# Attention weights of two batches transposed by TensorE in float32, those of two by DMA in float16, and all four worked off two heads at a time

## The chip, the cores and the metric

The kernel runs on one core of one Trainium2 chip. The metric is device time in microseconds (us), from the start of the program to its end. The kernel before took 1043.95 us, the median of three runs (1043.25 to 1050.18). The engines are named as in the profile: PE is TensorE, DVE is VectorE, ACT is ScalarE, POOL is GpSimd, SP is SyncE, which issues the DMAs.

## The reference

Three parts follow one another. The first is attention for B = 4 batches, H = 8 heads, S = 576 tokens and D = 64, with a memory term:

```python
scores = q @ k.T / sqrt(D)                    # causal: keys after the query get -1e9
a = exp(scores - scores.max(-1)); a /= a.sum(-1) + 1e-9
local = a @ v
q_p = where(q > 0, q, exp(q) - 1) + 1
mem_out = (q_p @ M_prev) / (q_p @ z_prev + 1e-6)
g = 1 / (1 + exp(-beta))                      # one number for each head
attn = g * mem_out + (1 - g) * local
```

Its output, 2304 tokens of 512 numbers, goes through two feed-forward layers with 512 inputs and 2048 hidden units: `(s * relu(x @ w_in)**2 + b) @ w_out`, and `(max(h, 0) + alpha * min(h, 0)) @ w_out` with `h = x @ w_in`. All inputs and the output are float32.

## The kernel before

**Order.** The program is not written in the order in which it runs. Each piece of work is handed to a planner (`Plan`, lines 68 to 254) by `op`, with an engine, a guessed duration, the keys it reads and writes, and a priority. `Plan.order` then lays out one fixed order for every engine's queue: whenever an engine is free it takes the ready piece of the highest priority. Attention comes ahead of feed-forward work (`ATT`, `MOE`, line 284), and the conversion of the first layer's weights ranks with batch 2 (`WP`, line 868). Some pieces may go to ACT or DVE (`either`, line 406), whichever is free first. The SBUF buffers are slots of 640 float32 columns, given out while the order is made: 15 for all (`NSLOT`, line 39), and 12 more in the room of the last four weight tiles, which batch 0 and the first weights use (`early`).

**Attention, batches 0 and 1** (`EXACT`, line 44; `pair`, line 628). Two heads lie one above the other in the 128 partitions, 64 rows each. The queries are cut into five chunks (`PAIRED`, line 33) in two sets, (0, 1) and (2, 3, 4) (`PSETS`). For each chunk PE makes the float32 scores of both heads (lines 680 and 692), DVE adds the mask and finds the largest (line 666), ACT takes the exponentials and their sums (line 658). Then the weights are scaled and split into a high float16 part on ACT (line 730) and what is left, the low part, on DVE (line 734). SP transposes both by a DMA (line 750), five of them for each pair of heads. PE multiplies them with the values, split in the same way (high by high, high by low, low by high, lines 761 to 765), into the lower and upper column half of a PSUM bank for the two heads, on top of the memory term (`remembered`, line 617, a float32 matmul against the identity). One copy brings the set out (lines 774 to 778).

**Attention, batches 2 and 3** (`head`, line 795). One head at a time, with keys and queries loaded twice, one copy above the other. Both are split into two float32r parts (lines 804 to 809), so that the 128 rows hold high and low keys and two matmuls make the scores (lines 813 and 814). Weights are again split into two float16 parts (lines 577 to 583), transposed by DMA (line 590) and multiplied (line 606). The memory term is written first (`recall`, line 780), and the local part is added onto it in two DVE instructions for each set (line 835).

For every pair of heads `values` (line 419) loads the values, sums their absolute values on ACT (line 435), spreads the sum by a small matmul (line 437) and makes the two float16 parts with that scale (lines 447 and 450). `features` (line 455) makes `q_p` and the memory term (lines 479 to 490).

**Feed-forward.** Layer 1 runs in seven blocks of tokens (512, 320, 320, then four of 288), layer 2 in five (four of 512, one of 256). Each block has 16 steps of 128 hidden units. A step has 12 matmuls into the hidden units (lines 945 to 947) and 12 into the output (lines 979 to 981), in two float32r parts with three products each. A block of layer 1 starts when the attention output of its tokens is stored (line 858) and loaded again (line 1035), and split (lines 1045 and 1047). The weights are loaded by step and converted by four DVE and one ACT instruction for each half (lines 889 to 905). PSUM has eight banks: four for the output sums, one for hidden units, two for scores and one for attention output (lines 339 to 343); in batch 0 the scores use six and the output two (line 393).

```python
ring = {"S": ["S0", "S1"], "O": ["O"]}[kind] + (spare[kind] if b == 0 else [])
```

Of the kernel before, what the change touches and what calls it, by code (L numbers as in the profile page):

```python
# [26 lines left out]
CHUNKS = [(0, 64), (64, 128), (192, 128), (320, 128), (448, 128)]  # L27
SETS = [(0, 1, 2), (3, 4)]

GROUPS = [[(0,), (1, 2)], [(3,), (4,)]]  # L30


PAIRED = [(128, 256), (128, 384), (128, 128), (128, 512), (64, 576)]
AT = [0, 128, 256, 384, 512]
PSETS = [(0, 1), (2, 3, 4)]
NC = len(CHUNKS)
NKB = 5
GW = 640
NSLOT = 15

XS = 7
RES = dict(t=0, fq=7, fe=1, fa=0, k=7, q=0, v=7, vf=6, p=1, w=2, xt=2, st=6, st2=4, wb=3, x=0)
W1GATE = 1
EXACT = (0, 1)
YS = 4
XF = 4
KG = 2
# [5 lines left out]
FLEX = 'x'  # L53
WP = 2.0
LIFT = 2.0 ** 14
# [4 lines left out]
class Slot:  # L60


    def __init__(self, reserve, early=False, size=1, above=0):
        self.reserve, self.early, self.size, self.above = reserve, early, size, above
        self.place, self.left, self.end = None, 0, 0.0


class Plan:
# [49 lines left out]
    def order(self):  # L118
# [12 lines left out]
        places = range(self.nslots + self.nextra)  # L131
# [19 lines left out]
        def spot(t, s):  # L151

            if s.early:
                for x in reversed(places[self.nslots + s.above:]):
                    if is_free(x, t) and (s.size == 1 or (x - self.nslots) % 3 < 2 and is_free(x + 1, t)):
                        return x
# [5 lines left out]
            return min(base, key=lambda x: place_free[x], default=None)  # L162

        gone = set()
        while len(out) < n:
# [21 lines left out]
            while avail[e]:  # L187
# [4 lines left out]
                new = [s for s in o[6] if s.place is None]  # L192
                if all(spot(t, s) is not None for s in new) and all(x in closed or not taken[x] and place_free[x] <= t for x in o[8]):
                    pick = c[1]
                    break
                closing.update(x for x in o[8] if x < self.nslots)
# [14 lines left out]
            closed.update(claim)  # L211
            for s in slots:
                if s.place is None:
                    s.place = spot(t, s)
                    for x in range(s.place, s.place + s.size):
                        taken[x] = True
# [13 lines left out]
            if nbytes:  # L230
                dma_free = max(dma_free + (110.0 if dur < 500 else 30.0), t + min(dur, 625.0) + 650.0) + nbytes / (360.0 if dur < 500 else 290.0)
                done[i] = dma_free + 900.0
# [35 lines left out]

def t_dve(n, rate=1.04, extra=0.0):
    return 69 + n * rate + extra  # L270
# [6 lines left out]
def build(tc, kd, kp, qd, vd, qp, mzd, beta8, sb2, win1, wout1, win2, wout2, alpha, outT):  # L277
# [8 lines left out]
    with tc.tile_pool(name="sb", bufs=1) as sb, tc.tile_pool(  # L286
# [30 lines left out]
        qh = sb.tile([128, S], F32R, name="qh")  # L317
        ql = sb.tile([128, S], F32R, name="ql")
        ks = sb.tile([128, S], F32R, name="ks")
        vsc = sb.tile([128, 2, 6], F32, name="vsc")  # L320
        allone = sb.tile([128, 128], F32, name="allone")
        mz = sb.tile([128, NP, MZ], F32, name="mz")
# [3 lines left out]
        mx = sb.tile([128, 2, NC + 1], F32, name="mx")  # L326
        sm = sb.tile([128, 2, NC + 1], F32, name="sm")
        mxp = sb.tile([128, 2, 10], F32, name="mxp")
        smp = sb.tile([128, 2, 10], F32, name="smp")
        nrm = sb.tile([128, 6], F32, name="nrm")  # L330
        wsc = sb.tile([128, H + 9 * NP], F32, name="wsc")
        bgc = sb.tile([128, H], F32, name="bgc")
        bsc = sb.tile([128, H + 9 * NP], F32, name="bsc")
# [23 lines left out]
        op("SP", 475, lambda: nc.sync.dma_start(out=bsc, in_=beta8), w=["bsc"], bytes_=512 * (H + 9 * NP), prio=-6)  # L357
# [12 lines left out]
        op("POOL", 300, lambda: nc.gpsimd.memset(sm, 1.0), w=[("sm", j, g) for j in range(2) for g in range(2)])  # L370

        op("POOL", 100, lambda: nc.gpsimd.memset(one, 1.0), w=["one"])

        def consts():

            A.activation(out=wsc, in_=bsc, func=AF.Exp)
            A.activation(out=bgc, in_=bsc[:, 0:H], func=AF.Exp, scale=-1.0)

        def consts2():
            V.tensor_scalar(out=wsc, in0=wsc, scalar1=1.0, scalar2=1.0 / LIFT, op0=ALU.add, op1=ALU.mult)  # L380
# [10 lines left out]
        cnt = {"ch": 0, "S": 0, "O": 0}  # L391

        spare = {"S": [("Y", d) for d in range(YS)], "O": ["H"]}

        def next_bank(b, kind):
            ring = {"S": ["S0", "S1"], "O": ["O"]}[kind] + (spare[kind] if b == 0 else [])
            cnt[kind] += 1
            return ring[cnt[kind] % len(ring)]


# [17 lines left out]

        def values(b, p):
# [3 lines left out]
            sv, sf = Slot(RES["v"], early), Slot(RES["vf"], early)  # L423
            tot, un, sc, gg = vsc[:, j, 0:1], vsc[:, j, 1:2], vsc[:, j, 2:3], vsc[:, j, 4:6]
            bk = next_bank(b, "S")
# [7 lines left out]
            op("SP", 475, lambda: nc.sync.dma_start(out=at(sv, n), in_=vd[b, p]),  # L433
               r=gate(b * H + 2 * p, KV, KV0), prio=-7 if b + p == 0 else None, w=[sv], bytes_=512 * n)
            op("ACT", t_act(n, 93, 180), lambda: A.activation(out=at(sf, n), in_=at(sv, n), func=AF.Abs, accum_out=tot),
               r=[sv], w=[sf, ("tot", j)])
            op("PE", 100, lambda: T.matmul(bank_of[bk][:, 0:1], allone, tot, start=True, stop=True),
# [3 lines left out]
                out=un, in0=bank_of[bk][:, 0:1], scalar1=2.0 ** -100, scalar2=LIFT ** -2, op0=ALU.max, op1=ALU.mult),  # L441
# [4 lines left out]
                out=gg, in0=bgc[:, 2 * p:2 * p + 2], scalar1=un, scalar2=None, op0=ALU.mult), r=[("un", j), "bgc"], w=[("gg", j)])  # L446
# [713 lines left out]
```

## Time and profile before

| | |
|---|---|
| median of three runs | 1043.95 us (1043.25 to 1050.18) |
| profiled execution | 1047.11 us, span 1045.2 us |
| PE busy | 998.5 us (96%) |
| DVE busy | 672.1 us (64%) |
| ACT busy | 498.7 us (48%) |
| POOL busy | 19.2 us (2%) |
| moved by DMA | 109.45 MB, 105 GB/s in the mean |

The span runs from the first instruction to the last. A busy share is an average over the whole span; the stages differ, so the rows below also cut it into stretches. Records of matmuls that follow one another overlap, since the next one starts while the last drains; a distance between two starts is what a matmul costs in a row of them. A float32 matmul shows as two records.

### The profile page before, as it was taken

What the parts mean: (1) busy time and instruction counts of PE and PEld (TensorE: products, weight loads), DVE (VectorE), ACT (ScalarE), POOL (GpSimd) and SP (SyncE); (2) the same over time, 40 slices, a digit from 0 to 9 for tenths busy, and PEclk for the clock granted to TensorE, in tenths of its full rate; (3) what the DMA queues carried; (4) which work ended last, traced back from release to release, by engine and by line L of the source; (5) the groups of instructions that cost most, each with busy time, mean ns of one, the idle gap of its engine ahead of it and who ended that gap; (6) DMA issues with size and microseconds to landing.
All of it is one profiled execution on the core that took longest, in us unless ns stands there. A gap on an engine that the chain in (4) does not pass through costs nothing.

```text
span 1045.2 us, 17420 instructions
## 1 busy us (share of the span) xinstructions
PE 998.5 (96%) x6544; PEld 866.4 (83%) x6544; DVE 672.1 (64%) x1607; ACT 498.7 (48%) x1198; POOL 19.2 (2%) x102
## 2 busy tenths in 40 slices
PE   6767999999999999999999999999999999999998
PEld 4544777768999999999999999888888888888898
DVE  6898998668678768667744367888434534433344
ACT  7774677568767777776644554222211211211111
POOL 1000000000000000000000000000000000000000
PEclk9865999998999999999999999999999999999999
DMA  5998856475456456455341134332200200100010
GB/s 166 202 222 261 243 134 196 112 187 128 116 126 134 117 131 155 91 133 128 74 169 41 64 121 164 101 122 90 81 1 1 71 1 1 40 1 1 1 41 21
DMA packets 150500, 109.45 MB, mean 105 GB/s; under 512 B 118160, under 2 KB 125328, under 8 KB 150416
## 3 DMA queue, kind: packets, MB, share of 16 engines
q1 hardware_dynamic: 150416, 108.34, 38.7%
q8 instruction: 51, 0.84, 0.3%
q14 instruction: 33, 0.27, 0.1%
HBM read 65.85 MB, written 14.16 MB: 77 GB/s over the span
## 4 chain that ended last, share of the span: by engine, by line
PE 79%; DVE 5%; DMA 5%; ACT 2%; issue 1%; SPq 1%; ACTq 0%; DVEq 0%
PE yb L979 12%; PE yb L980 12%; PE yb L981 12%; PE hb L945 7%; PE hb L946 7%; PE hb L947 7%; PE sp L945 3%; PE sp L947 3%; PE sp L946 3%; PE ob L606 2%; PE ob L945 2%; PE ob L947 2%; PE ob L946 2%; DMA pool<-pool 1%; PE sp L813 1%
## 5 line engine op out<-in xcount | busy, mean ns | idle before, releaser
L979 PE MATMUL yb<-gr,wt 128*128 128x288 f32 (+4 forms) x608 | 204.8, 337 | 0.2 <-ACT pool L1004 0.2
L980 PE MATMUL yb<-gr,wt 128*128 128x288 f32 (+4 forms) x608 | 200.3, 330 | 0.0
L981 PE MATMUL yb<-gr,wt 128*128 128x288 f32 (+4 forms) x608 | 200.1, 329 | 0.0
L945 PE MATMUL hb<-xr,wt 128*128 128x288 f32 (+3 forms) x528 | 176.6, 334 | 0.7 <-ACT gt L959 0.5
L946 PE MATMUL hb<-xr,wt 128*128 128x288 f32 (+3 forms) x528 | 171.1, 324 | 0.0
L947 PE MATMUL hb<-xr,wt 128*128 128x288 f32 (+3 forms) x528 | 170.9, 324 | 0.0
L967 ACT CAST gr<-gt 128x288 fp32r<-128x288 f32 (+3 forms) x152 | 75.1, 494 | 141.0 <-DVE gt L965 134.2
L968 DVE TENSOR_TENSOR gr<-gt,gr 128x288 fp32r<-128x288 f32 (+3 forms) x152 | 81.2, 534 | 76.3 <-ACT gr L967 75.2
L979 PEld LDWEIGHTS yb<-gr,wt 128*128 128x128 f32 x608 | 114.6, 189 | 12.0 <-issue 3.3
L981 PEld LDWEIGHTS yb<-gr,wt 128*128 128x128 f32 x608 | 114.6, 188 | 8.5
L980 PEld LDWEIGHTS yb<-gr,wt 128*128 128x128 f32 x608 | 114.7, 189 | 7.8
L945 PEld LDWEIGHTS hb<-xr,wt 128*128 128x128 f32 x528 | 100.2, 190 | 12.1 <-issue 5.3
L947 PEld LDWEIGHTS hb<-xr,wt 128*128 128x128 f32 x528 | 100.1, 190 | 5.8
L946 PEld LDWEIGHTS hb<-xr,wt 128*128 128x128 f32 x528 | 100.4, 190 | 5.0
L959 ACT ACTIVATE gt<-hb 128x288 f32<-128x288 f32 (+2 forms) x112 | 49.7, 444 | 98.2 <-PE hb L947 95.4
L967 ACT CAST qh<-mz 128x512 fp32r<-128x512 f32 (+1 forms) x40 | 23.1, 578 | 143.7 <-DVE mz L965 143.6
L981 PE MATMUL yb<-ql,wt 128*128 128x512 f32 (+1 forms) x160 | 59.6, 372 | 0.0
L945 PE MATMUL sp<-xr,wt 128*128 128x512 f32 (+1 forms) x160 | 59.4, 371 | 0.0
L947 PE MATMUL sp<-xr,wt 128*128 128x512 f32 (+1 forms) x160 | 59.4, 371 | 0.0
L946 PE MATMUL sp<-xr,wt 128*128 128x512 f32 (+1 forms) x160 | 59.4, 371 | 0.0
L980 PE MATMUL yb<-qh,wt 128*128 128x512 f32 (+1 forms) x160 | 59.2, 370 | 0.0
L979 PE MATMUL yb<-qh,wt 128*128 128x512 f32 (+1 forms) x160 | 59.1, 369 | 0.1
(306 smaller groups left out, 1823.4 us busy)
## 6 DMA issues: line engine op xcount, KB each, us to landing
pool<-win SPq DMA_DIRECT2D x19, 512.0 KB, 4.4
pool<-wout SPq DMA_DIRECT2D x15, 512.0 KB, 3.7
room<-wout SPq DMA_DIRECT2D x14, 512.0 KB, 4.7
room<-win SPq DMA_DIRECT2D x11, 512.0 KB, 4.1
pool<-y SPq DMA_DIRECT2D x18, 256.0 KB, 3.6
out_t<-pool SPq DMA_DIRECT2D x16, 256.0 KB, 2.0
pool<-qd SPq DMA_DIRECT2D x12, 288.0 KB, 3.2
pool<-kd SPq DMA_DIRECT2D x10, 288.0 KB, 3.4
```

The lines of the kernel that those rows point to most:

```text
L606: T.matmul(obk[:, q0 - o0:q0 - o0 + nq], W[:, kb, pw], P[:, x, 0:nq], start=(first and kb == x == 0), stop=False, skip_group_check=True)
L813: T.matmul(sp, qh[:, q0:q0 + 128], ks[:, k0:k0 + kn], start=True, stop=False)
L945: T.matmul(H_, W_h, X_h, start=(d == 0), stop=False)
L946: T.matmul(H_, W_h, X_l, start=False, stop=False)
L947: T.matmul(H_, W_l, X_h, start=False, stop=(d == KD - 1))
L959: op("ACT", t_act(n, 50), lambda: A.activation(out=t_, in_=H_, func=AF.Relu), r=[hk, "gr"], w=[tk], prio=-1)
L967: op("ACT", t_act(n), lambda: A.copy(out=G_h, in_=t_), r=[tk], w=[("gh", gj)], prio=-1)
L968: op("DVE", t_dve(n), lambda: V.tensor_tensor(out=G_l, in0=t_, in1=G_h.bitcast(F32), op=ALU.subtract), r=[tk, ("gh", gj)], w=[("gl", gj)], ...
L979: T.matmul(Y, W_h, G_h, start=(f == 0), stop=False)
L980: T.matmul(Y, W_l, G_h, start=False, stop=False)
L981: T.matmul(Y, W_h, G_l, start=False, stop=(f == KF - 1))
```

## The change

- `WHOLE = (0, 1)`: in batches 0 and 1 the weights stay float32. They are scaled in place (ACT or DVE), transposed by PE in blocks of 128 columns into a PSUM bank, up to four blocks at a time, and copied back (ACT or DVE) over the place they came from. The products are float32 against the values as loaded. The split of the values, their sum and the scale fall away there.
- Batches 2 and 3 are worked off by `pair` too, two heads at a time, with two float16 parts, DMA transposes and three products, as batches 0 and 1 were before. `scores`, `turn`, `products`, `remembered`, `recall` and `head` are gone, and so are the doubled keys and queries.
- The memory term is brought in by matmuls with `is_transpose`, in the same instruction group as all products of a set.
- PSUM banks are no longer dealt round: the planner gives them out like slots (`Bank`), all eight in batch 0 and three later. A piece of PE work also takes the slot that its exponentials will fill (`room_for`).
- `NSLOT` is 17 instead of 15; the reserves, guessed durations and DMA rates of the planner change; layer 2's first weight load, and no longer its first token load, claims the slots that layer 2's split tokens take over.

```diff
-EXACT = (0, 1)
+WHOLE = (0, 1)
+class Bank(Slot):
+    def __init__(self, banks):
+        super().__init__(0)
+        self.banks = banks
+        def bank_for(b):
+            return Bank(range(8) if b == 0 else range(3))
+        def bank_at(bk):
+            return banks[bk.place - NSLOT - 3 * XF]
...
+            if b in WHOLE:
+                return sv                    # values: no sum, no parts
...
+        def turn_whole(b, g, j, cs, ch0, sp, sw, weights_of):
...
+                    either("x", t_act(nk, 93, 93), lambda p_c=p_c, sc=sc, nk=nk: A.activation(
+                        out=p_c(0, nk), in_=p_c(0, nk), func=AF.Copy, scale=sc),
+                        t_dve(nk, 0.52, 60), lambda p_c=p_c, sc=sc, nk=nk: V.tensor_scalar(
+                        out=p_c(0, nk), in0=p_c(0, nk), scalar1=sc, scalar2=None, op0=ALU.mult), r=[("sm", j, g, col)], w=wk)
...
+                    for k0 in range(0, nkb, 3 if nkb == 5 else 4):
+                        n = min(3 if nkb == 5 else 4, nkb - k0)
+                        bk = bank_for(b)
+                        def mm(p_c=p_c, k0=k0, n=n, bk=bk):
+                            for i in range(n):
+                                T.transpose(bank_at(bk)[:, 128 * i:128 * i + 128], p_c(128 * (k0 + i), 128), ident)
...
+                        either("x", t_act(128 * n, 50), lambda p_t=p_t, k0=k0, n=n, bk=bk: A.copy(
+                            out=p_t(k0, n), in_=bank_at(bk)[:, 0:128 * n]),
+                            t_dve(128 * n), lambda p_t=p_t, k0=k0, n=n, bk=bk: V.tensor_copy(
+                            out=p_t(k0, n), in_=bank_at(bk)[:, 0:128 * n]), r=[bk], w=[(s, c, k0, "t")])
...
+                turned = (turn_whole if b in WHOLE else turn_parts)(b, g, j, cs, ch0, sp, sw, weights_of)
+                ok = bank_for(b)
+                def mm(cs=cs, turned=turned, o0=o0, ok=ok):
+                    obk = bank_at(ok)
+                    for c in cs:
+                        nq = CHUNKS[c][0]
+                        r = 128 - nq
+                        T.matmul(obk[:, AT[c] - o0:AT[c] - o0 + nq], at(sa, 2 * D * NC)[r:, 2 * D * c:2 * D * c + 2 * D],
+                                 ident[r:, r:], is_transpose=True, start=(c == cs[0]), stop=False, skip_group_check=True)
...
+                        for kb in range(nkb):
+                            for w, k in ((0, kb),) if b in WHOLE else ((0, kb), (1, kb), (0, nkb + kb)):
                                 for odd in (1, 0):
+                                    _, p_t, y = turned[odd, c]
+                                    T.matmul(obk[D * odd:D * odd + D, AT[c] - o0:AT[c] - o0 + nq], W[:, kb, odd, w],
+                                             p_t(k)[:, y:y + nq], start=False, stop=False, skip_group_check=True)
...
-                if b in EXACT:
-                    pair(b, p, sp_, sa, sf, xt)
-                else:
-                    recall(b, p, sa, xt)
-                    head(b, 2 * p, sf, xt)
-                    head(b, 2 * p + 1, sf, xt)
+                pair(b, p, sp_, sa, sv, xt)
```

`turn_parts` holds the splitting and the DMA transposes that `pair` had before (lines 712 to 752).

## Rows read from the trace of the kernel before

**Rows 1.** The page, part 1: busy us (share of the span) and instructions of each engine.
```profile
PE 998.5 (96%) x6544; PEld 866.4 (83%) x6544; DVE 672.1 (64%) x1607; ACT 498.7 (48%) x1198; POOL 19.2 (2%) x102
```

**Rows 2.** Stretches: length, then each engine's busy us (instructions), PE clock, DMA share, GB/s.
```profile
0.00:67.20 67.20, 48.37 (x454) 32.78 (x455) 54.51 (x189) 53.32 (x145) 3.09 (x17) 0.90 0.80 194
67.20:95.50 28.30, 16.25 (x122) 11.35 (x121) 24.53 (x66) 15.70 (x37) 0.20 (x1) 0.51 0.95 253
...
105.10:226.00 120.90, 118.22 (x781) 87.35 (x781) 100.95 (x252) 83.09 (x186) 0.61 (x3) 1.00 0.61 166
226.00:245.10 19.10, 14.51 (x115) 11.38 (x115) 12.54 (x38) 12.41 (x33) 0.84 (x5) 0.82 0.67 202
...
545.00:1045.20 500.20, 496.20 (x2628) 428.54 (x2628) 258.73 (x426) 120.10 (x235) 0.00 (x0) 1.00 0.15 51
```

**Rows 3.** Timeline, end of batch 0: start us, us, engine, line, operation [idle before].
```profile
67.06 0.20 ACT L658 ACTIVATION_READ_ACCUMULATOR room<-yb,mxp 128x1 f32 x1
...
73.21 0.81 DVE L734 SCALAR_TENSOR_TENSOR room<-room,smp,room 128x576 f16<-128x576 f32 x1
...
72.00 5.59 SPq L750 DMA_TRANSPOSE room<-room  x3
...
83.89 0.33 SPq L858 DMA_DIRECT2D x<-room  x1
...
87.37 0.42 SPq L1035 DMA_DIRECT2D poolx<-x  x1
...
95.54 0.79 PE L945 MATMUL hb<-xr,wt 128*128 128x512 f32 x1
```

**Rows 4.** Stretch 0 to 67.2 us, instructions of line 734 alone (busy on DVE).
```profile
0.00:67.20 67.20, 16.13 (x31) 0.90 0.80 194
```

**Rows 5.** The same stretch, instructions of line 730 alone (busy on ACT).
```profile
0.00:67.20 67.20, 15.47 (x31) 0.90 0.80 194
```

**Rows 6.** Single lines: engine, operation xcount: ns min/median/max, first and last start, shapes.
```profile
L450 DVE SCALAR_TENSOR_TENSOR poolx<-poolx,vsc x4: 855/866/881, 59.9 to 487.6; 128x640 f16<-128x640 f32 x4
L447 ACT ACTIVATE poolx<-poolx,vsc x4: 828/829/832, 53.1 to 484.7; 128x640 f16<-128x640 f32 x4
L435 ACT ACTIVATE poolx<-poolx x4: 727/732/732, 35.0 to 460.0; 128x640 f32<-128x640 f32 x4
L891 DVE TENSOR_SCALAR pool<-pool x31: 416/421/428, 49.9 to 725.2; 128x512 int32<-128x512 int32 x31
L1013 DVE COPY pool<-yb x10: 424/690/692, 732.7 to 1041.7; 128x512 f32<-128x512 f32 x8, 128x256 f32<-128x256 f32 x2
```

**Rows 7.** Timeline of PE, batch 1: bundles of attention matmuls at full clock.
```profile
206.59 0.49 PE L680 MATMUL sp<-pool,poolx 64*128 64x128 f32 x4
...
210.64 1.13 PE L680 MATMUL sp<-pool,poolx 64*128 64x512 f32 x4
...
215.82 0.88 PE L617 MATMUL ob<-ident,pool 128*128 128x128 f32 x6 [0.18 <-ACT poolx L774]
216.63 0.70 PE L692 MATMUL sp<-pool,poolx 64*64 64x288 f32 x4
...
227.65 1.03 PE L764 MATMUL ob<-poolx,pool 128*64 128x128 f16 x30 [1.21 <-DMA poolx<-pool]
...
229.07 0.66 PE L764 MATMUL ob<-pool 128*64 128x64 f16 x30 [0.39 <-DMA pool<-poolx]
```

**Rows 8.** Timeline of PE, batch 2: scores and products of one head between feed-forward matmuls.
```profile
290.27 0.38 PE L813 MATMUL sp<-ks,qh 128*128 128x288 f32 x1
290.49 0.30 PE L814 MATMUL sp<-ks,ql 128*128 128x288 f32 x1
290.62 0.31 PE L945 MATMUL hb<-xr,wt 128*128 128x320 f32 x1
...
291.32 0.73 PE L606 MATMUL ob<-poolx,pool 128*128 128x128 f16 x10
291.86 0.40 PE L945 MATMUL hb<-xr,wt 128*128 128x320 f32 x1
```

More of the change, by code (lines that the diff above doesn't have):

```diff
@@ L130, in order @@
         done = [0.0] * n
-        places = range(self.nslots + self.nextra)
+        places = range(self.nslots + self.nextra + 8)
         place_free = [0.0 for _ in places]
@@ L162, in spot, with take @@
             return min(base, key=lambda x: place_free[x], default=None)
+        def take(t, new):
+            for k, s in enumerate(new):
+                s.place = spot(t, s)
+                if s.place is None:
+                    for u in new[:k]:
+                        for x in range(u.place, u.place + u.size):
+                            taken[x] = False
+                        u.place = None
+                    return False
+                for x in range(s.place, s.place + s.size):
+                    taken[x] = True
+            return True
         gone = set()
@@ L191, in order @@
                 o = self.ops[c[1]]
[L192 to L196, printed above, removed]
+                if all(x in closed or not taken[x] and place_free[x] <= t for x in o[8]):
+                    closed.update(o[8])
+                    if take(t, [s for s in o[6] if s.place is None]):
+                        pick = c[1]
+                        break
+                else:
+                    closing.update(x for x in o[8] if x < self.nslots)
                 skipped.append(c)
@@ L210, in order @@
             eng, dur, fn, deps, prio, nbytes, slots, late, claim = self.ops[i]
[L211 to L216, printed above, removed]
             if e == "PE":
@@ L389, in build @@
            r=["ident"], w=["ident"])
[L391 to L398, printed above, removed]
+        cnt = {"ch": 0}
+        banks = [sbank[0], sbank[1], obank, hbank] + ybank
+        def bank_for(b):
+            return Bank(range(8) if b == 0 else range(3))
+        def bank_at(bk):
+            return banks[bk.place - NSLOT - 3 * XF]
         def gate(hg, ahead, ahead0):
@@ L593, in products @@
-        def products(g, part, parts, turned, sf, obk, ok, first=False):
-            pw, c = part
-            q0, nq, nk, pk, p_c, ch = parts[part]
-            tk, p_t = turned[part]
-            nkb = c + 1
-            o0 = CHUNKS[SETS[g][0]][0]
-            def mm():
-                P = p_t()
-                W = at(sf, 2 * NKB * 2 * D, FP16).rearrange("p (n h e) -> p n h e", h=2, e=2 * D)
-                for kb in range(nkb):
-                    for x in (kb, nkb + kb):
-                        T.matmul(obk[:, q0 - o0:q0 - o0 + nq], W[:, kb, pw], P[:, x, 0:nq],
-                                 start=(first and kb == x == 0), stop=False, skip_group_check=True)
-            op("PE", 2 * nkb * t_b(nq), mm, r=[tk, sf], w=[ok], prio=ATT + ch * 10 + 1)
@@ L677, in pair @@
+                    room_for = [(weights_of(c, odd)[0], c, "s") for odd in range(2)]
                     if c < NC - 1:
@@ L846, in attention @@
                 plan.lean = VLEAN
-                sf = values(b, p)
+                sv = values(b, p)
                 plan.lean = FLEAN
```

453 lines of the change are left out of this document (166 added, 287 removed).

## Prediction

> **What bounds the kernel now.** I read the whole span first, then the stretches, then the few rows at the joints between them. Over the span PE is busy 96% of the time [rows 1]. That is an average over stages with different limits, so the stretches decide [rows 2]. From 545 us to the end PE is busy 496 of 500 us at full clock, on feed-forward matmuls alone. From 105 to 226 us, where the first feed-forward block shares PE with batch 1, it is busy 118 of 121 us. Behind 105 us, then, the time is PE work, and a microsecond of PE work taken out or put in there is a microsecond of the kernel. Two places are different. Up to 67 us DVE (54.5 of 67.2 us) and ACT (53.3) set the pace while PE has room. And between 226 and 245 us PE is idle 4.6 us and runs at a mean clock of 0.82.
>
> The joint at the start is in [rows 3]. The last exponentials of batch 0 end at 67.3 us; its last low weight part is made on DVE at 73.2 to 74.0; SP issues three transposes in 72.0 to 77.6; the last store of batch 0 is issued at 83.9, the load of the same rows at 87.4, and the first feed-forward matmul starts at 95.5. From there on PE never runs dry for long. So the change has two sides: what it does to 95.5 us, and what it does to PE work afterwards.
>
> **Start, batch 0.** Removed up to 67.2 us: 31 low parts on DVE, 16.1 us [rows 4]; four splits of the values, 0.87 us each, 3.5 us [rows 6]; 31 high parts on ACT, 15.5 us [rows 5]; four high value parts of 0.82 us, 3.3 us [rows 6]; and the sums of absolute values that go with them, 0.73 us each, 2.9 [rows 6]. DVE falls from 54.5 to 34.9, ACT from 53.3 to 31.6. Added, on whichever of the two is free: 31 scalings in place, at 0.42 us for 512 columns if DVE does them [rows 6], some 0.3 each, 9.3 us, or the 15.5 of ACT above; and the copies of the transposed blocks out of PSUM. A pair has 25 blocks of 128 columns, 3200 columns in 10 copies. A 512-column copy takes 0.69 us [rows 6], so a pair costs 4.2 us and the 31 of 36 parts done by then 14.5. The sum over both engines is 90 to 96 us, 45 to 48 for each, against 54.5: the exponentials of the last pair end some 8 us sooner, near 59.
>
> Then the tail. Before, 16.6 us lie between the last exponential and the store. Instead of parts, SP issues and landings there are five scalings (2 us over two engines), 15 transposes with six copies (about 3 us), the products (five blocks at 0.45 and five of half the columns at 0.22 at half clock, 3.4 us) and a copy out of 0.6: 9 us, 7.6 less. Store to first matmul I leave at its 11.6 us, although SP no longer has 20 transposes of batch 0 in its queue, ahead of these loads among others. Start: 8 + 8 = **-16 us**, first matmul near 79.5. Ends: 0 (below: PE holds it back) and -25 (DVE and ACT at their 45 us, SP free).
>
> **PE work in batch 0 has to fit under that.** A pair costs PE now, from [rows 7], each bundle counted with its drain: scores 0.49 for 128 keys and 1.13 for 512, the two sizes between them in proportion, with the two halves of the last chunk at 0.70: 4.6; products 1.03 + 1.03 + 0.66 = 2.7; five float32 matmuls that bring in the memory term 1.5 (three take 0.88); the features are five more of 130 columns, 1.5; a small one for the values, put at 0.3. That is 10.6, less some 0.1 drain for each of 15 bundles: 9.1 us. The change adds 25 transposes, takes the float32 products for float16 ones, and passes the memory term as transposes. No row shows a float32 transpose on PE. The nearest row is a float32 128x128 matmul, two records in the bundle of three [rows 7], some 0.22 us without the drain; a float16 one takes 0.054 (ten in [rows 8], 0.54 to the next start). A transpose moves the data once and must load 128 float32 columns each time, so I take one record, 0.11 us: 2.75 us for a pair, with ends 1.4 and 5.6. The float32 products of two heads lie in the two column halves. The float16 ones there overlap, 30 in 1.03 us, and the float32 scores of the last chunk, in two column and two row halves, overlap too: two matmuls of 288 columns in 0.70 us, where at the 1.7 ns a column of the 0.22 one after the other needs 0.98. I take overlap: 10 blocks at 0.22 and 5 at 0.11, 2.75 us (end: 5.5, without it), instead of 2.6. The memory term falls by half, -0.65; the value sums go, -0.15. With four more bundles a pair, at 0.1, PE pays **+2.5 us a pair** (ends +1 and +8). Batch 0 then needs 4 x 11.6 = 46 us of PE at full clock, 51 at the 0.90 of the first 67 us [rows 2]: with the first wait of 4.6 that is 56, and the last store is due at 68: it fits, with little to spare. (The clock was mostly 2.4 GHz up to 67 us, and 1.2 GHz from there to 95 almost throughout [rows 2].)
>
> The Trainium skill, in its page "TensorE: Matmul & The Clock Gate" (Terms), has a transpose mode four times as fast for float32, which would make a block 0.056 us instead of my 0.11. No run here shows it; by that rule a pair pays 1.4 us less and batch 1 ends 5.6 us sooner than in my sum.
>
> **Batch 1** stands behind 95.5 us, where PE is the bound, so its four pairs cost 4 x 2.5 = **+10 us** (ends +4, +32). DVE and ACT lose work here too, but that is under PE. The new wait is that the products of a set are one instruction group that waits for all copies of the set; behind it in PE's queue stand feed-forward matmuls, which the order can put ahead. If that cover is gone, a set waits about a copy and its signal, 1 us, eight times.
>
> **Batches 2 and 3** go from one head at a time to two. Removed on PE for two heads: scores 2 x 2 x 1600 columns at 0.46 ns (0.13 us from the start of one of 288 columns to the next start in [rows 8]) = 2.9 us; 60 float16 products at 0.054 = 3.2; the memory term 1.1. Added: scores 4.2, products 2.5, memory term as transposes 0.55. That is 7.2 against 7.3. What falls is the number of bundles, 24 to 8 a pair, and entering one costs 0.09 us (the first score matmul of 288 columns takes 0.22 to the next start, the following one 0.13 [rows 8]): at most 16 x 0.09 x 8 = -11 us. The float32 pairs start slowly themselves, which the bundle durations may hide, so I take **-4 us** (ends -11, +6). DVE, ACT, POOL and DMA work removed here (ks and ql splits, the half-height additions, 7 MB of doubled keys and queries) lies under PE and counts nothing.
>
> **The hole at 226 to 245 us** is 4.6 us idle and 0.18 x 14.5 = 2.6 us of clock, 7.2 in all: block 0 runs out before batch 1 delivers. Batch 1 has less DVE, ACT and SP work in front of it, but also more PE. Half: **-4 us** (ends -7, +4).
>
> Layer 2's weights now take their slots earlier; PE was busy 99% there and I cost it at nothing, since loads and conversions lie under half a block of matmuls.
>
> **Sum:** -16 + 10 - 4 - 4 = -14 us. The profiled execution took 1047.1 us (span 1045.2, 1.9 around it), 3.2 above the median of the three runs, 1043.95; the change carried over gives 1030.
>
> **Rivals.** (a) *PE's float32 price.* If the products in the two column halves don't overlap, a pair pays x = 2.8 us more. Batch 1 then costs 11 more; batch 0 needs 4 x 14.4 = 58 us of PE, 64 at 0.90 and 69 with the first wait, which can't be packed without gaps before 68, so the start is some 5 later: -14 + 16 = +2, 1046. With transposes at the full 0.22 as well, x = 5.6: batch 1 +22, batch 0 4 x 17.2 = 69, 76 at 0.90, start 14 later, -14 + 36 = +22, **1066**. It decides from about x = 2.4 on, where the sum is zero. For: no float32 product with 128 rows in a column half is in the trace. Against: the 0.70 row. (b) *The clock stays low in the start.* For: it was 0.51 from 67 to 95 us, with PE busy 16 of 28 us [rows 2]. Against: up to 67 us it was 0.90, with PE less busy than it will be. At a mean of 0.6, batch 0 needs 46 / 0.6 = 77 us of PE, 82 with the first wait, the last store comes at 83 as before, and the sum is -16 of the start short: +2, **1046**; at 0.5 throughout it needs 92, the store is 14 later than before, +16, 1060. The Trainium skill says of PE transposes (same page, Part 4, PE-mode transpose) that the full clock does not engage for them; by that rule this rival is the likelier, and no row here bears on it, because no transpose is there. (c) *The start gains more.* No DMA between weights and products, fewer slots for each pair: start -25, hole closed, bundles -11: -25 + 10 - 11 - 7 = -33, **1011**. (d) *The start is bound elsewhere*, by loads (DMA share 0.80 and 0.95 in the first two stretches [rows 2]) or the weights' conversions, which take over the freed DVE: start -4, sum -2, 1042. Against: it is transposes that held SP before the last store, three of them for 5.6 us [rows 3].
>
> **Chances.** Forecast 0.50 (its own range 1020 to 1042), a 0.10, b 0.14, c 0.12, d 0.09, the rest 0.05. Faster by over 1% is under 1033.5, slower above 1054.4; 1% is about what a measurement of this kernel can tell from no change. The forecast puts 0.36 below 1033.5 and 0.14 within 1%. With c and some of the rest, faster is 0.50. With d, half of a and 0.09 of b, same is 0.36; the other halves and the rest make slower 0.14. The range 1011 to 1054 leaves out the far ends of a and b and the tail of c, about 2 in 10.
>
> **What would show it.** First feed-forward matmul near 79 us, DVE and ACT below 48 us busy up to the last exponentials of batch 0, no transpose issue on SP in batches 0 and 1: the start is right. Float32 transposes starting 0.11 us apart and the two heads' products overlapping: +2.5 is right; 0.22 or products one after another is (a). A clock row of 0.5 to 0.7 before the first block is (b). A stretch near 220 us without idle PE closes the hole. If the span behind the first feed-forward matmul is longer than before by more than 10 us, my PE prices failed; if it is shorter, the bundles were worth more than I gave them.

## The result, and the profile after

The changed kernel takes **1017.42 us** (median of six runs, 1016.51 to 1017.99) against 1044.56 for the kernel before, timed beside it (1042.71 to 1050.18): a ratio of 0.973 (95% interval 0.971 to 0.976), 27 us less. The time lies in the predicted range, but below the forecast's own 1020 to 1042. The sum said -14; the sections below look for the other 13.

The page's first part, which answers to [rows 1]: PE does as much as before, in a shorter span; DVE, ACT and POOL lose 88, 37 and 14 us.

```profile
PE 997.8 (98%) x6648; PEld 846.0 (83%) x6648; DVE 584.1 (58%) x1389; ACT 461.3 (45%) x1113; POOL 5.1 (0%) x29
```

The end of batch 0 in the timeline, which answers to [rows 3]: the last exponentials, a bundle of transposes, the last store, the load of the same rows and the first feed-forward matmul.

```profile
54.05 0.26 ACT L641 ACTIVATION_READ_ACCUMULATOR poolx<-sp,mx 128x1 f32 x1
...
56.37 0.33 PE L551 MATMUL yb<-ident,poolx 128*128 128x128 f32 x1 [2.10 <-ACT poolx L536]
...
64.01 0.33 SPq L754 DMA_DIRECT2D x<-room  x1
...
66.14 0.33 SPq L934 DMA_DIRECT2D pool<-x  x1
...
74.55 0.78 PE L844 MATMUL hb<-xr,wt 128*128 128x512 f32 x1
```

The last exponentials end at 54.3 us (67.3 before), the store is issued at 64.0 (83.9), the first feed-forward matmul starts at 74.55 (95.54). No transpose stands in SP's queue there. The stretches, in the columns of [rows 2]: up to the last exponentials, from there to the first matmul, two stretches of [rows 2] again, and layer 2.

```profile
0.00:54.40 54.40, 47.83 (x438) 33.90 (x438) 46.57 (x177) 44.85 (x132) 3.05 (x18) 1.00 0.48 161
54.40:74.50 20.10, 13.83 (x94) 10.96 (x95) 19.17 (x58) 12.76 (x32) 0.00 (x0) 0.75 0.77 258
...
105.10:226.00 120.90, 120.90 (x823) 90.44 (x821) 89.63 (x246) 83.23 (x205) 0.36 (x2) 1.00 0.37 112
226.00:245.10 19.10, 19.10 (x131) 16.54 (x123) 12.08 (x39) 13.60 (x36) 0.20 (x1) 1.00 0.39 109
...
545.00:1015.70 470.70, 467.05 (x2412) 398.26 (x2410) 246.12 (x404) 105.87 (x202) 0.00 (x0) 1.00 0.16 51
```

The clock is 1.00 up to 54 us, with the transposes in it, and the hole at 226 to 245 us is gone: 19.10 us busy of 19.10. To compare kernels I cut every trace at its first feed-forward matmul: what lies behind it is one stretch, whose length less PE's busy time is PE's idle time. Before, then after:

```profile
0.00:95.54 95.54, 64.66 (x577) 44.14 (x577) 79.08 (x254) 69.01 (x180) 3.29 (x18) 0.78 0.84 212
95.54:1045.20 949.66, 933.85 (x5969) 822.30 (x5968) 593.03 (x1354) 429.65 (x1018) 15.88 (x84) 0.99 0.35 94
```

```profile
0.00:74.55 74.55, 61.70 (x533) 44.91 (x533) 65.80 (x234) 57.61 (x163) 3.05 (x18) 0.93 0.56 187
74.55:1015.70 941.15, 936.13 (x6118) 801.06 (x6116) 518.29 (x1156) 403.70 (x950) 2.02 (x11) 1.00 0.28 78
```

The start gives 21.0 us and the stretch behind it 8.5 of the span, where idle PE falls from 15.8 to 5.0 us. The same cut follows for all kernels. The median and its ratio come from all runs, each timed beside the kernel before (whose median was 1044.56 to 1045.51 there); the last three columns, in us, come from the one profiled execution, which lies up to 2.6 us from its median.

| kernel | median us | ratio to before (95%) | start | behind | PE idle behind |
|---|---|---|---|---|---|
| before | 1044.56 | | 95.54 | 949.66 | 15.8 |
| after | 1017.42 | 0.973 (0.971 to 0.976) | 74.55 | 941.15 | 5.0 |
| pairs alone, old order | 1059.04 | 1.014 (1.011 to 1.018) | 92.63 | 963.77 | 20.4 |
| parts in all batches | 1034.14 | 0.991 (0.988 to 0.993) | 87.95 | 943.25 | 15.5 |
| float32 in batch 0 | 1020.59 | 0.978 (0.975 to 0.980) | 74.33 | 943.77 | 14.0 |
| float32 in all batches | 1041.86 | 0.998 (0.997 to 0.999) | 74.18 | 965.42 | 5.6 |
| old guesses | 1026.33 | 0.982 (0.980 to 0.984) | 83.72 | 942.68 | 10.1 |
| 15 slots | 1029.90 | 0.986 (0.984 to 0.988) | 78.10 | 950.30 | 14.8 |
| banks dealt round | 1043.21 | 0.998 (0.997 to 1.000) | 86.05 | 955.15 | 16.9 |
| work back on DVE | 1030.94 | 0.987 (0.985 to 0.989) | 85.03 | 943.27 | 7.2 |
| two pairs of batch 1 | 1018.60 | 0.976 (0.972 to 0.979) | 73.59 | 942.91 | 8.4 |
| last pair of batch 1 | 1011.89 | 0.968 (0.966 to 0.970) | 72.82 | 935.58 | 6.7 |
| third pair of batch 1 | 1023.12 | 0.979 (0.975 to 0.982) | 73.27 | 947.93 | 13.2 |

### The profile page after: what moved, and what is told of

Same layout as the page of the kernel before. It is cut to its first block, busy times and chain, and to the rows that moved or that the text cites. A ratio compares the mean times of both kernels' runs of the same rounds, so it can differ in the third digit from the quotient of the medians.

```text
span 1015.7 us, 16933 instructions
## 1 busy us (share of the span) xinstructions
PE 997.8 (98%) x6648; PEld 846.0 (83%) x6648; DVE 584.1 (58%) x1389; ACT 461.3 (45%) x1113; POOL 5.1 (0%) x29
## 3 DMA queue, kind: packets, MB, share of 16 engines
q1 hardware_dynamic: 85520, 86.05, 29.3%
## 4 chain that ended last, share of the span: by engine, by line
PE 95%; DVE 3%; ACT 1%; DMA 0%; issue 0%; SPq 0%; ACTq 0%; DVEq 0%
PE yb L878 14%; PE yb L880 13%; PE yb L879 13%; PE hb L844 9%; PE hb L845 8%; PE hb L846 8%; PE sp L846 3%; PE sp L845 3%; PE sp L844 3%; PE sp L716 2%; PE sp L663 2%; PE ob L845 2%; PE ob L844 2%; PE ob L846 2%; PE ob L663 1%; PE sp L551 1%
## 5 line engine op out<-in xcount | busy, mean ns | idle before, releaser
L878 PE MATMUL yb<-gr,wt 128*128 128x512 f32 (+4 forms) x768 | 264.6, 345 | 0.1
L880 PE MATMUL yb<-gr,wt 128*128 128x512 f32 (+4 forms) x768 | 259.6, 338 | 0.0
L879 PE MATMUL yb<-gr,wt 128*128 128x512 f32 (+4 forms) x768 | 259.4, 338 | 0.0
L878 PEld LDWEIGHTS yb<-gr,wt 128*128 128x128 f32 x768 | 144.4, 188 | 23.8 <-issue 8.1
L880 PEld LDWEIGHTS yb<-gr,wt 128*128 128x128 f32 x768 | 144.5, 188 | 14.7 <-DVE gr L867 0.2
L879 PEld LDWEIGHTS yb<-gr,wt 128*128 128x128 f32 x768 | 144.6, 188 | 13.4
L866 ACT CAST gr<-mz 128x512 fp32r<-128x512 f32 (+1 forms) x40 | 23.1, 578 | 158.0 <-DVE mz L864 157.9
L845 PE MATMUL sp<-xr,wt 128*128 128x512 f32 (+1 forms) x160 | 59.3, 371 | 0.0
L648 DVE CUSTOM_DVE_ANT_0 sp<-sp,mask 128x384 f32<-128x384 f32 (+4 forms) x81 | 40.8, 514 | 25.4 <-PE sp L663 14.8
L859 ACT ACTIVATE gt<-gt 128x288 f32<-128x288 f32 (+2 forms) x112 | 53.5, 478 | 2.4
L867 DVE TENSOR_TENSOR gr<-mz,gr 128x512 fp32r<-128x512 f32 (+1 forms) x40 | 25.6, 639 | 25.3 <-ACT gr L866 25.3
```

Of the source, the lines that this page charges most:

```text
L648: op("DVE", t_dve(kn, 1.04, 60 if before is not None else 0), lambda: V.tensor_tensor_reduce(out=bank_at(bk)[:, 0:kn], in0=bank_at(bk)[:, ...
L845: T.matmul(H_, W_h, X_l, start=False, stop=False)
L859: op("ACT", t_act(n), lambda: A.activation(out=t_, in_=t_, func=AF.Square), w=[tk], prio=-1)
L866: op("ACT", t_act(n), lambda: A.copy(out=G_h, in_=t_), r=[tk], w=[("gh", gj)], prio=-1)
L867: op("DVE", t_dve(n), lambda: V.tensor_tensor(out=G_l, in0=t_, in1=G_h.bitcast(F32), op=ALU.subtract), r=[tk, ("gh", gj)], w=[("gl", gj)], ...
L878: T.matmul(Y, W_h, G_h, start=(f == 0), stop=False)
```

## The experiments: which part of the change gives what

**Parts in all batches.** On the changed kernel, float16 parts and DMA transposes everywhere:

```diff
-WHOLE = (0, 1)
+WHOLE = ()
```

> The changed kernel with all four batches in two float16 parts and DMA transposes (no float32 weights anywhere); banks, slots, planner and the two-heads form stay as changed. Theory A (the gain at the start comes from batch 0's float32 weights: less DVE and ACT work and no DMA between weights and products): the start goes back by most of its 21 us, PE work falls by some 10 us in batch 1, idle and low clock come back by some 10: 1035 to 1045. Theory B (the gain comes from the freer PSUM banks, the slots and the planner's new durations): 1025 or less.

**Float32 in batch 0 alone:**

```diff
-WHOLE = (0, 1)
+WHOLE = (0,)
```

> The changed kernel with float32 weights in batch 0 alone; batch 1 in two float16 parts with DMA transposes. By PE work alone (batch 1's float32 form costs 2.5 us of PE a pair, and PE is the bound there) it is some 10 us faster than the changed kernel: 1005 to 1010. If the float32 form of batch 1 pays for itself in idle time and clock between the start and 245 us (17 us less of them after the change than I had given 4 for), it is 1017 to 1027.

**Float32 in all four:**

```diff
-WHOLE = (0, 1)
+WHOLE = (0, 1, 2, 3)
```

> The changed kernel with float32 weights in all four batches. Theory A with PE as the bound behind the start: 8 pairs at 2.5 us more, 1035 to 1040, with nothing idle to win back. Theory B (the form of the transposes hardly matters): 1012 to 1022.

**The other way round:** the kernel before with batches 2 and 3 by pairs, and nothing else.

```diff
-EXACT = (0, 1)
+EXACT = (0, 1, 2, 3)
```

> The kernel before with batches 2 and 3 also worked off two heads at a time (float16 parts, DMA transposes, old banks and planner durations); batches 0 and 1 as they were. My term for that part was -4 us with ends -11 and +6: 1040 (1033 to 1050), with the start still near 95 us. If a large part of the gain behind the start came from here, 1030 or less.

Measured: 1034.14, 1020.59, 1041.86 and 1059.04 us. The first lies just under the range of theory A, the second in that of its second reading, the third 2 us above theory A, the fourth 9 us above its range. Read as a way from before to after, the steps are +14.5 (pairs in the old order), -24.9 (all the rest of the new order, that is slots, banks, reserves and guesses, and the memory term as transposes), -13.6 (float32 in batch 0) and -3.2 (float32 in batch 1). So on this way the float32 transposes bring 17 of the 27 us, and the new order, less what the pairs cost in the old one, 10. The two are not a sum that holds in any order: with the banks dealt round, below, float32 and all else of the change take 1043.21 us, and almost nothing of the 27 is left.

Float32 in batch 0 acts on the start alone: 87.95 to 74.33, and behind it 943.25 to 943.77. Float32 in batches 2 and 3 shows PE's bare price, since there PE hardly waits in either kernel (idle 5.0 and 5.6): 965.42 - 941.15 = 24.3 us for eight pairs, 3.0 a pair. Batch 1 should cost 12 by that; it gave 2.6 (943.77 to 941.15). The difference is the hole. The stretch of it with parts in batch 1:

```profile
200.00:220.00 20.00, 10.72 (x97) 8.42 (x95) 10.29 (x31) 9.40 (x25) 0.00 (x0) 0.66 0.69 189
```

PE is busy 10.7 of 20 us there, at a clock of 0.66; the changed kernel is busy 20.00 of 20 in it at 1.00. So closing the hole was worth about 12 + 2.6 = 14.6 us, an estimate, since the 12 is the price from batches 2 and 3. Of it 9.0 us are PE's idle time behind the start (14.0 to 5.0); I put the rest to the low clock. My sum had 4 for a hole, but for the smaller one of the kernel before.

## The experiments: what the order is worth

Each undoes one thing on the changed kernel. **The guesses** of DMA rates and of PE's time for the scores of a pair, as they were:

```diff
-                dma_free = max(dma_free + (110.0 if dur < 500 else 30.0), t + min(dur, 625.0) + 650.0) + nbytes / (330.0 if dur < 500 else 160.0)
+                dma_free = max(dma_free + (110.0 if dur < 500 else 30.0), t + min(dur, 625.0) + 650.0) + nbytes / (360.0 if dur < 500 else 290.0)
...
-    return 200 + 4 * n / 2.4
+    return 2 * t_f(n)
```

> The changed kernel, but the planner gets the guesses of before for a transfer's rate and for a pair of score matmuls. All four batches in the old order cost 14 us more in idle time and clock when batches 2 and 3 were moved to pairs, and the new banks, slots and guesses with the same float16 form are 25 us faster than that. If the guesses make the 25, this run is at 1030 or above; if banks or slots make them, within 5 us of the changed kernel (1013 to 1022).

**The slots:**

```diff
-NSLOT = 17
+NSLOT = 15
```

> The changed kernel with 15 slots instead of 17. If the two more slots make the 25 us, 1030 or above; if the guesses or the banks, 1014 to 1022.

**The banks**, dealt round in a fixed turn as before:

```diff
-            return Bank(range(8) if b == 0 else range(3))
+            ring = {"S": [0, 1], "O": [2]}[kind] + ({"S": [4, 5, 6, 7], "O": [3]}[kind] if b == 0 else [])
+            cnt[kind] += 1
+            return Bank((ring[cnt[kind] % len(ring)],))
```

> The changed kernel with PSUM banks dealt round as before (two for scores and transposes, one for the output; six and two in batch 0), instead of given out when free. If the free choice of a bank makes the 25 us, 1030 or above, with PE idle behind the start; if the guesses or the slots, 1014 to 1022.

**DVE's work in batch 0:** one more DVE operation for every chunk, 36 in all, that writes a float16 part which nobody reads; the values are computed as in the changed kernel. The last line makes the transposes of the chunk wait for it.

```diff
+                    if b == 0:
+                        ss = Slot(RES["p"], True)
+                        op("DVE", t_dve(nk, 1.04, 60), lambda p_c=p_c, sc=sc, nk=nk, ss=ss: V.scalar_tensor_tensor(
+                            out=at(ss, GW, FP16)[:, 0:nk], in0=p_c(0, nk), scalar=sc, in1=p_c(0, nk),
+                            op0=ALU.mult, op1=ALU.subtract), r=wk[0:1] + [("sm", j, g, col)], w=[ss, (s, c, "b")])
+                        wk = wk + [(s, c, "b")]
```

> The changed kernel with one more DVE instruction for each chunk of weights in batch 0 (36 in all, the size of the low part that was removed; its output goes to an unused slot and nothing else is left out). If the start is shorter because DVE and ACT have less to do, the first feed-forward matmul goes from 74.5 us to 80 to 86 and the time to 1023 to 1030, since half of the 18 us can be moved to ACT. If it is shorter because no DMA lies between weights and products, the start moves by at most 3 us: 1017 to 1021.

Measured: 1026.33, 1029.90, 1043.21 and 1030.94 us, that is +8.9, +12.5, +25.8 and +13.5. None of the three edits of the order is free, as I had costed them, and none alone makes the 25 us that the three expectations share out. They act in different places. The old guesses cost almost wholly in the start (83.72 for 74.55). With 15 slots most lies behind it, and two waits explain about half: the last attention output is stored at 504.9 us instead of 437.7, and ahead of the last block of layer 1, in the stretch 500 to 560 us, PE waits for its converted tokens (line 943). The waits of PE there (engine, tile and line that waited, what it waited for: us, times, longest):

```profile
PE hb L844 <- ACT xr L943: 3.9, 1, 3.9
PE hb L844 <- ACT gt L858: 1.2, 1, 1.2
```

The changed kernel has PE busy 60.00 of 60 us in that stretch, the one of 15 slots 54.80. Dealt banks cost most: 11.5 us in the start and 14.0 behind it. Block 0 of the feed-forward ends at 214 us, block 1 begins at 244, and the stretch between shows the hole of before again, larger. The longest waits of PE from 74 to 260 us:

```profile
PE sp L552 <- ACT pool L537: 3.0, 1, 3.0
PE sp L664 <- ACT pool L642: 2.7, 2, 2.3
PE sp L507 <- ACT pool L642: 1.7, 1, 1.7
PE sp L676 <- ACT pool L642: 1.7, 1, 1.7
PE sp L552 <- ACT pool L560: 1.6, 3, 0.7
```

Most are waits of scores, features (line 507) and transposes (line 552) for exponentials (line 642), scalings (line 537) and copies (line 560), in other words for what reads the dealt bank or makes its next tenant. That the fixed turn is what makes them wait is my reading: the edit also parts the three banks again into two and one, and no run gave a bank more or less.

In the fourth, DVE's own work grows from 65.80 to 76.41 us ahead of the first feed-forward matmul (the added operations take 19.0, but scalings and copies go over to ACT), and that matmul comes 10.5 us later:

```profile
0.00:85.03 85.03, 66.28 (x538) 46.33 (x539) 76.41 (x256) 63.76 (x174) 3.20 (x19) 0.89 0.45 151
85.03:1028.30 943.27, 936.04 (x6112) 801.44 (x6110) 524.57 (x1171) 401.12 (x940) 2.44 (x10) 1.00 0.28 79
```

10.6 us more on DVE, 10.5 us more of start. But the transposes also wait for the added operation, so the run doesn't tell DVE's load from a longer way for each chunk. The last exponentials and the last store of batch 0, first in this run, then with parts in all batches:

```profile
62.53 0.21 ACT L647 ACTIVATION_READ_ACCUMULATOR poolx<-sp,mx 128x1 f32 x1
...
73.79 0.33 SPq L760 DMA_DIRECT2D x<-room  x1
```

```profile
59.13 0.21 ACT L641 ACTIVATION_READ_ACCUMULATOR poolx<-yb,mx 128x1 f32 x1
...
72.58 0.38 SPq L754 DMA_DIRECT2D x<-room  x1
```

Here 8.4 of the 10.5 us lie ahead of the last exponentials (62.7 for 54.3). With parts in batch 0 the start is 13.6 us longer than with float32 there (87.95 for 74.33), but only 5.1 of them lie ahead of the last exponentials (59.3 for 54.2); 4.8 lie between these and the store (13.2 for 8.4) and 3.7 between the store and the first matmul (15.4 for 11.7). So the start is not shorter by DVE's and ACT's work alone: more than half of what float32 gives batch 0 lies behind the exponentials, 4.8 us of it where the parts go through DMA.

## The experiments: why batch 1 gains, and which pair

`b in WHOLE` is replaced by a condition on batch and pair. **The last two pairs of batch 1** in float32:

```diff
-            if b in WHOLE:
+            if b == 0 or b == 1 and p >= 2:
```

> Float32 weights for batch 0 and, of batch 1, for its last two pairs of heads alone; its first two go by float16 parts and DMA transposes. What it tells apart is why float32 in batch 1 pays although it adds PE work (with parts in the whole of batch 1 the time was 1020.59, with float32 in the whole of it 1017.42). Theory: what opens the hole near 210 us is the way from the last exponentials of batch 1 through parts, SP and landing to the products, so it is the last pairs that must be free of it; the first two then give back 2 x 2.6 us of PE and the hole stays closed: 1017.4 - 5 = 1012. Rival: it is the whole batch's work on DVE, ACT and SP that makes it late, evenly by pair; then half of the 14.5 us of idle PE and low clock comes back and 5 of PE work goes: 1019 to 1020.

**The last pair alone** (`p == 3`):

> The same with float32 weights, in batch 1, for its last pair of heads alone. Theory (the tail of the last pair): three pairs give back 2.6 us of PE each and the hole stays closed, 1017.4 - 8 = 1010. Rival (the whole batch's work, evenly): three quarters of the 14.5 us come back, less 8: 1020 to 1021. If 1012 comes with two pairs and 1020 with one, it is the last two that count.

**The third pair in its place** (`p == 2`):

> Float32 weights for batch 0 and for one pair of heads of batch 1, as in the version of 1011.89, but for its third pair in place of its last. With the last pair in float32 the last store of batch 1 was issued at 200.7 us, with parts throughout at 211.0; of these 10 us, 3 lie between the last exponentials and the store (9.9 for 12.9) and 7 ahead of them. Theory one, the tail of the last pair: only that pair's way through SP counts, the last store comes near 210 again, the hole stays open, and the time is that of parts throughout and 2.6 us of PE: 1021 to 1023. Theory two, the order: a float32 pair takes fewer slots and no transposes, and lets its neighbours go ahead whichever pair it is; the last store comes near 203, and the time is 1012 to 1015.

Measured: 1018.60, 1011.89 and 1023.12 us. One float32 pair at the end gives 8.7 us against parts throughout, the same pair one place earlier costs 2.5. So the even rival is out for one pair (1020 to 1021): which pair it is decides. But two pairs at the end came out just under where the even rival had them (1019 to 1020), not at the 1012 of the theory. The timeline of parts throughout batch 1: the first and the last exponentials of the last pair, the three DMA transposes on SP, the first product, the store, the load, the first matmul of block 1.

```profile
182.76 0.47 ACT L641 ACTIVATE pool<-sp,mx 128x256 f32<-128x256 f32 x1 [2.06 <-DVE mx L648]
...
198.10 0.20 ACT L641 ACTIVATION_READ_ACCUMULATOR pool<-sp,mx 128x1 f32 x1
...
202.36 1.36 SPq L608 DMA_TRANSPOSE pool<-poolx  x1
203.82 1.59 SPq L608 DMA_TRANSPOSE poolx<-poolx  x1
205.51 1.56 SPq L608 DMA_TRANSPOSE pool<-pool  x1
...
207.77 0.26 PE L716 MATMUL sp<-poolx,pool 128*64 128x128 f16 x1 [2.60 <-DMA poolx<-poolx]
...
211.00 0.33 SPq L754 DMA_DIRECT2D x<-pool  x1
...
214.38 0.38 SPq L934 DMA_DIRECT2D pool<-x  x1
...
220.24 0.41 PE L844 MATMUL hb<-xr,wt 128*128 128x320 f32 x1
```

Block 0 ends at 200.7 us, and there is nothing else for PE until 220.24 but this pair and the first work of batch 2, which has itself to wait. With the last pair in float32 (line numbers four higher):

```profile
173.07 0.48 ACT L645 ACTIVATE poolx<-sp,mx 128x256 f32<-128x256 f32 x1 [0.41 <-DVE mx L652]
...
191.12 0.20 ACT L645 ACTIVATION_READ_ACCUMULATOR poolx<-ob,mx 128x1 f32 x1
...
198.30 1.31 PE L720 MATMUL sp<-pool,poolx 128*64 128x128 f32 x20
...
200.69 0.33 SPq L758 DMA_DIRECT2D x<-poolx  x1
...
207.64 0.41 PE L848 MATMUL hb<-xr,wt 128*128 128x320 f32 x1
```

From the last exponential to the products it is 7.0 us (191.3 to 198.3) for 9.5, to the store 9.4 for 12.7. So of the 10.3 us by which the store comes sooner, the tail gives 3.3; the other 7 lie ahead of it, since the last pair's exponentials begin at 173.1 instead of 182.8. The same first exponentials and the store, with two pairs and then with the third pair alone:

```profile
183.95 0.48 ACT L645 ACTIVATE poolx<-sp,mx 128x256 f32<-128x256 f32 x1 [1.38 <-DVE mx L652]
...
209.46 0.32 SPq L758 DMA_DIRECT2D x<-pool  x1
```

```profile
185.10 0.48 ACT L645 ACTIVATE poolx<-sp,mx 128x256 f32<-128x256 f32 x1 [2.75 <-DVE mx L652]
...
214.79 0.33 SPq L758 DMA_DIRECT2D x<-poolx  x1
```

The tail is short wherever the last pair is float32 (8.1 us with two pairs) and long wherever it has parts (13.1 with the third). That much is shown. But the last pair starts early only where it alone is float32 or the whole batch is (166.8 us), and late in the other three; with two pairs that takes back what the short tail gives. Why the planner's order starts it sooner or later, no run shows.

The two-pair version misses its forecast of 1012 by 6.6 us. PE idles 8.4 us behind the start, 1.7 more than with one pair. Of the 7.3 us between the two stretches behind the start (942.91 and 935.58), 3.0 is the price of a pair; the rest goes with the late last pair and stays as open as that. The version with the last pair alone beats both kernels: 1011.89, a ratio to before of 0.968 (0.966 to 0.970).

## The experiment on the clock

240 more transposes of the identity stand ahead of all other PE work.

```diff
+        def warm():
+            for i in range(240):
+                T.transpose(ps_at(wbank)[:, 0:128], ident, ident)
+        op("PE", 240 * 110, warm, r=["ident"], w=["warm", wbank], prio=-100)
```

> The changed kernel with 240 more float32 transposes of the identity, 128 x 128, ahead of all other PE work, one after the other; only these are in the stretch. What it tells apart is whether PE's clock rises to 2.4 GHz under transposes alone. If it does, the stretch shows a granted clock of 0.5 at its beginning and 1.0 behind that, starts 0.22 us apart at first and 0.11 later, about 30 us in all, and the first feed-forward matmul comes some 20 us later than 74.5. If it does not, the clock is 0.5 to the end of the stretch, with 0.22 us between starts and 53 us in all, and the first feed-forward matmul comes some 45 us later.

One execution: 1043.22 us, first feed-forward matmul at 103.55, 29 later (some 20 were expected). The stretches with nothing but transposes on PE:

```profile
3.40:6.40 3.00, 2.96 (x14) 2.96 (x15) 0.76 (x1) 1.26 (x2) 0.08 (x1) 1.00 1.00 352
6.40:9.40 3.00, 3.00 (x29) 3.00 (x28) 0.68 (x4) 1.61 (x4) 0.00 (x0) 1.00 0.98 348
9.40:12.40 3.00, 3.00 (x30) 3.00 (x29) 1.29 (x2) 1.26 (x2) 0.00 (x0) 1.00 0.23 71
12.40:31.00 18.60, 18.60 (x173) 18.60 (x171) 0.00 (x0) 0.00 (x0) 0.00 (x0) 1.00 0.01 2
```

173 in 18.6 us is 0.1075 us each at a granted clock of 1.00, that is 2.4 GHz. In the first 3 us they start twice as far apart, as at 1.2 GHz, although the row says 1.00 there too; the record of the clock and the pace differ in these 3 us, and I trust the pace. The 27.9 us of transposes, to which the rest of PE's work waits, make 29 of start.

## Why the prediction was right, and where it was wrong

**The whole: in the range, not by the sum.** The range holds because it reached down to rival (c), at 1011; the forecast's own range was missed. Behind the start the sum said +2 us (10 - 4 - 4) and the span gave -8.5; in the start it said -16 and got -21.0. That is 10.5 and 5.0 us, of which some 2.5 go off because the profiled execution of the kernel before lay that much above its median: the 13 us that the sum missed.

**The bound, and the sign: right.** Behind the start PE sets the time, and the float32 price was read well. A transpose is one record, 0.11 us, and the products of two heads overlap. The timeline of batch 1 in the changed kernel shows both:

```profile
186.14 1.03 PE L551 MATMUL sp<-ident,poolx 128*128 128x128 f32 x8
187.01 0.49 PE L551 MATMUL ob<-ident,poolx 128*128 128x128 f32 x3
...
189.66 0.58 PE L702 MATMUL sp<-ident,pool 128*128 128x128 f32 x3
190.17 1.89 PE L716 MATMUL sp<-poolx,pool 128*64 128x128 f32 x40
191.99 0.50 PE L878 MATMUL yb<-gr,wt 128*128 128x512 f32 x1
```

Eight transposes in 0.87 us are 0.109 each; 40 records (two each for ten blocks of two heads, line 716) in 1.82 us are 0.182 with the last five blocks of half the columns, against the 0.22 and 0.11 of the sum, 0.165 in the mean. The memory term takes 0.51 us for three. A pair costs 3.0 in the runs for the predicted 2.5. So rival (a) is out, and the 0.70 us row that spoke against it pointed the right way. The Trainium skill's transpose mode, four times as fast for float32 ("TensorE: Matmul & The Clock Gate", Terms), doesn't show: 0.109, not 0.056.

**Rivals (b) and (d): out.** The clock was 1.00 up to 54 us with all but 15 of batch 0's 100 transposes in that stretch, and the last experiment shows it under transposes alone. The sign that I had named for (b), a row near 0.5, did come after 54 us (last section), but the mean of the start was 0.93. The Trainium skill says in the same page (Part 4, PE-mode transpose) that the full clock does not engage for them; no run here agrees, the pace of 0.1075 us is that of 2.4 GHz. Rival (d), a start bound by loads or conversions, had -4 us where -21.0 came.

**Start: -16 predicted, -21.0 measured.** By its own steps: the exponentials end 13.0 us sooner (predicted 8), from there to the store it is 9.7 for 16.6 (predicted 9), from the store to the first matmul 10.5 for 11.6 (predicted no change). The first step was too small, and not by its work: 36 scalings took 15.6 and 40 copies 17.3 us over both engines, which for 31 of 36 chunks is 13.4 and 14.9, against 9.3 to 15.5 and 14.5. I took the saved busy time of DVE as the gain and so held its 12.7 us of idle time fixed (67.2 - 54.5 [rows 2]); it fell to 7.8 (54.4 - 46.6), which is the 5 us between 8 and 13. Two edits that I had costed at nothing bear on it: dealt banks put the start back by 11.5 us, the old guesses by 9.2.

**Batch 1: +10 predicted, some +12 by the price of a pair.** The term was right, and so was that it stands behind the start, where PE pays.

**The hole: -4 predicted; about -15 measured against parts in batch 1.** This term was mis-sized. I counted 7.2 us between 226 and 245 us and halved them for the two effects that I saw there; the changed kernel has none of them left, so against the kernel before it is -7.2. And the hole of before was no bound: without float32 in batch 1 the kernel with the faster start has 9.3 us idle in 20, and a lower clock. I did not follow the last pair of batch 1 to the first matmul of block 1. Part of that way is three DMA transposes of 1.4 to 1.6 us each on SP with their landing, the same tail that I had used for the start (16.6 us); the larger part is when the last pair starts, which stays open.

**Batches 2 and 3 by pairs: -4 predicted, +14.5 alone in the old order.** Behind the start 14.1 us, of which PE's idle time is 4.6 (15.8 to 20.4) and PE's busy time the other 9.5. With slots, banks, guesses and the transposed memory term beside it (parts in all batches) the stretch is 6.4 us shorter than before, near the -4 and the -2.6 of the memory term in batch 1; that run holds many edits at once, so this may be chance. I had taken a shorter stretch as a sign that the bundles were worth more than I gave them; no run shows that. I had costed the bundles on PE and not asked whether 15 slots and three dealt banks carry two heads at a time; which of them the pairs lack wasn't separated.

**Banks, slots, guesses: nothing predicted; +25.8, +12.5, +8.9 us when each is undone.** This is the step that failed: the sum has no term for them. The prediction's one sentence on the order, that "loads and conversions lie under half a block of matmuls", speaks of layer 2's weights alone. The parts of these figures overlap; together with the memory term they were -24.9 in the float16 form. Rival (c) (start -25, hole closed, 1011) was the nearest case. Of its reasons, the way through DMA is shown for the tails of batches 0 and 1 (4.8 us and 3.3 us); that a pair takes fewer slots was not tested by itself.

## What to carry to other kernels

Price an edit of a hand-planned order (banks, slots, guessed durations) as a term with bounds, not at nothing: much of its price is the idle time that shows in the stretches where engines wait for one another in turn, and the busiest engine's own idle time there is not fixed. Where one stage feeds the next, follow the last piece to its landing; a dearer way for that piece alone (one pair of batch 1 here) was the best of the mixes tried. And price a resource stretch by stretch: the same 3 us of PE a pair bought a shorter start in batch 0, came back almost four times over in the last pair of batch 1 (943.77 - 935.58 + 3.0 = 11.2 us), and were lost in batches 2 and 3.

## What the runs showed of the hardware

Float32 transposes by PE run at full clock and start 0.1075 to 0.109 us apart for 128x128. The granted clock fell twice in the changed kernel, to 0.51, each time behind a wait of PE (2.1 us before 56.4, 1.7 us before 66.5):

```profile
57.50:61.00 3.50, 3.36 (x17) 2.96 (x16) 2.79 (x9) 2.27 (x5) 0.00 (x0) 0.51 0.85 309
61.00:67.70 6.70, 4.69 (x54) 3.10 (x52) 6.48 (x18) 3.97 (x10) 0.00 (x0) 1.00 0.42 127
67.70:78.10 10.40, 8.25 (x30) 6.79 (x30) 10.40 (x32) 6.16 (x18) 0.00 (x0) 0.51 0.76 278
```

PE was busy 3.36 of 3.5 and 8.25 of 10.4 us while the clock was low, so busy time alone doesn't show a low clock. With the last pair of batch 1 alone in float32, 1.6 us of idle PE between 200 and 220 us, in three waits of 0.4 to 0.7 us, left it at 1.00: not every wait brings it down.
